# Window attention, forward and backward, on one core: transposes by DMA, shared score matmuls and a hand-ordered pipeline over four tiles

## The chip, the cores and the metric

The kernel runs on one core of one Trainium2 chip. The metric is the device time of the program in microseconds (us). The kernel before takes 3114.75 us (median of four runs, 3114.29 to 3115.95).

The engines are named as the profile names them: PE multiplies matrices (PEld is its weight loading), DVE and ACT do vector work, POOL and SP (SyncE) here mostly issue DMAs. "Evicting" a tile means copying a PSUM tile to SBUF, with a cast to bf16 where the PSUM tile is float32.

## The reference, cut to what matters

```python
# x, grad_out: (1, 256, 256, 384) bf16; wqkv: (384, 1152); wo: (384, 384); windows of 8 x 8 tokens
xw  = windows(x)                                  # 1024 windows of 64 tokens
q, k, v = split(xw @ wqkv)
p   = softmax(einsum('bqc,bkc->bqk', q, k) * 384**-0.5)
out = einsum('bqk,bkc->bqc', p, v) @ wo
# returned: out, and the gradients of x, wqkv and wo for grad_out
```

Both kernels fold the weights: with A = scale Wq Wk^T the scores are x A x^T, and with B = Wv Wo the output is P (x B). A tile is 128 tokens, that is two windows. Four tiles make a quad, and there are 128 quads. dS is the gradient of the scores, dP that of the probabilities. The weight gradients are accumulated as G and F from x^T U and x^T W, with U = dS^T x and W = P^T grad.

## The kernel before

The framework's scheduler orders the instructions of each engine. Per quad the kernel does this (cut):

```python
# x and grad of each tile are transposed on PE, and copied out of PSUM by DVE
for m in range(CK):
    nc.tensor.transpose(ps_xdT[:, 0, m*P:(m+1)*P], x_tok[:, m*P:(m+1)*P], ident[:])
for m in range(CK):
    nc.tensor.transpose(ps_xdT[:, 1, m*P:(m+1)*P], do_tok[:, m*P:(m+1)*P], ident[:])
nc.vector.tensor_copy(out=xdT_quad[:, :, :, bi*P:(bi+1)*P], in_=ps_xdT[:].rearrange(...))
# ... projections yT, xBT for the quad (512 columns), xBT transposed back on PE ...
for stage in (stage_f1, stage_f2, stage_b1, stage_b2, stage_b3):
    for bi in range(QUAD):
        stage(bi)          # softmax, output, dP, dS, U, W, one tile at a time
# stage_b3: dx of a tile, nine matmuls of 384 columns
for A_sb, srcT, o0 in ((A1_sb, uvwT_sb, 0), (A2_sb, uvwT_sb, P), (A3_sb, wT_sb, 0)):
    for mc in range(CK):
        nc.tensor.matmul(ps_dx[:], lhsT=srcT[:, mc, o0:o0+P], rhs=A_sb[:, mc, :], ...)
# ... after 16 tiles: G_acc and F_acc += x^T U, x^T W (ps_dw) ...
```

## Time and profile before

| what | value | view |
|---|---|---|
| span | 3115.0 us | page |
| PE / DVE / ACT busy | 98% / 65% / 49% | page, part 1 |
| PE's share of the chain that ended last | 88% | page, part 4 |
| one quad in the middle of the run | about 24 us | span over 128 quads, less the ends |

From the page: busy time and instructions of each engine, then two rows of the 40 time slices (the TensorE clock granted, and the busy share of the DMA engines, both in tenths).

```profile
PE 3041.1 (98%) x23935; PEld 1867.8 (60%) x23935; DVE 2020.5 (65%) x6758; ACT 1527.4 (49%) x3981; POOL 614.2 (20%) x1034
...
PEclk9999999999999999999999999999999999999999
DMA  4222222212222122222222221222212222222211
```

PE is nearly always busy and its clock is full. That alone does not say that PE is used well, because matmuls are pipelined and overlap. (The Trainium skill, "Trainium Kernel Development and Optimization", section "Performance Expectations", calls matmul busy time a bad metric for that very reason.) So look at the chain of waits, followed back from the last instruction, as shares of the span:

```profile
PE 88%; DVE 4%; issue 4%; ACT 3%; DMA 0%; ACTq 0%
```

At nearly every step PE's own previous matmul is what held the next one up. Two merged rows of the timeline (start, length, engine, line, operation, count) show its real pace:

```profile
1505.06 0.97 PE L316 MATMUL ps_dx<-A_sb,uvwT_sb 128*128 128x384 bf16 x5
...
1506.45 0.33 PE L210 MATMUL ps_xB<-ident,xBT_sb 128*128 128x128 bf16 x3
```

One matmul of 384 columns lasts 326 ns, but five take 0.97 us: they start (0.97 - 0.326) / 4 = 161 ns apart. Transposes of 128 columns start about 56 ns apart. These spacings, not the lengths, are what a removed matmul is worth. The transposes that the change moves to DMA stand in these groups (count, then busy us and mean ns of one, then the engine's idle time before them):

```profile
L180 PE MATMUL ps_xdT<-ident,x_tok 128*128 128x128 bf16 x1536 | 196.6, 219 | 2.2 <-DVE A_sb L118 0.3 <-DVE xdT_quad L183 0.3
L182 PE MATMUL ps_xdT<-ident,do_tok 128*128 128x128 bf16 x1536 | 185.5, 219 | 0.0
L183 DVE COPY xdT_quad<-ps_xdT 128x768 bf16<-128x768 bf16 x512 | 278.8, 549 | 6.9 <-PE ps_xdT L182 2.6
```

### The profile page before, as it was taken

Reading aid. Unit: us, or ns where it says so; the run is one execution under the profiler, and the core shown is the slowest. Engines: PE = TensorE matmul, PEld = TensorE weight load, DVE = VectorE, ACT = ScalarE, POOL = GpSimd, SP = SyncE. Lnnn points to the kernel's source line nnn. Section 1 sums busy time; section 2 is a strip of 40 time slices with the busy share of each in tenths; the row PEclk is TensorE's granted clock in tenths of the full one; section 3 lists DMA queues with packets and bytes.
Section 4 is the critical chain, followed back from the end, with each engine's and each line's share of the span. In section 5 each row is a group of like instructions: output and inputs, shape, how many; then the busy total and the mean of one; then the engine's idle time right before and its main releaser. Section 6 shows DMA issues by size and latency. Waiting matters only on the chain.

```text
span 3115.0 us, 64454 instructions
## 1 busy us (share of the span) xinstructions
PE 3041.1 (98%) x23935; PEld 1867.8 (60%) x23935; DVE 2020.5 (65%) x6758; ACT 1527.4 (49%) x3981; POOL 614.2 (20%) x1034
## 2 busy tenths in 40 slices
PE   8999999999999999999999999999999999999998
PEld 5565656666666656666566656566665656656564
DVE  6666766667666666666666666766666666667665
ACT  4445544445444454444554444544445444455443
POOL 4122111122111121111211212211112111121100
PEclk9999999999999999999999999999999999999999
DMA  4222222212222122222222221222212222222211
GB/s 129 68 63 64 71 69 69 70 52 76 68 70 69 52 76 69 70 68 60 65 71 70 71 66 54 76 68 70 70 53 74 68 70 69 62 65 71 58 33 40
DMA packets 206716, 208.43 MB, mean 67 GB/s; under 512 B 49216, under 2 KB 181056, under 8 KB 206400
## 3 DMA queue, kind: packets, MB, share of 16 engines
q0 software_dynamic: 65536, 101.25, 12.2%
q1 hardware_dynamic: 140464, 102.76, 11.2%
q8 instruction: 187, 3.06, 0.4%
q14 instruction: 129, 1.06, 0.1%
q10 hardware_dynamic: 400, 0.29, 0.0%
HBM read 101.84 MB, written 101.84 MB: 65 GB/s over the span
## 4 chain that ended last, share of the span: by engine, by line
PE 88%; DVE 4%; issue 4%; ACT 3%; DMA 0%; ACTq 0%
PE ps_dx L316 24%; PE ps_dw L331 13%; PE ps_p L190 8%; PE ps_p L196 8%; PE ps_t L300 5%; PE ps_W L282 4%; PE ps_w L305 4%; PE ps_xB L210 3%; PE ps_dP L259 3%; PE ps_U L277 3%; PE ps_S L216 3%; PE ps_out L248 2%; DVE xdT_quad L183 2%; PE ps_xdT L180 2%; PE ps_xdT L182 2%
## 5 line engine op out<-in xcount | busy, mean ns | idle before, releaser
L316 PE MATMUL ps_dx<-A_sb,uvwT_sb 128*128 128x384 bf16 x3072 | 703.6, 326 | 0.1
L175 POOL DMA_DIRECT2D do_tok<-in_grad_out_dram x512 | 300.6, 588 | 1429.1 <-PE ps_w L305 1247.3
L302 ACT CAST uvwT_sb<-ps_t 128x512 bf16<-128x512 f32 (+1 forms) x1024 | 498.9, 487 | 85.8 <-PE ps_t L300 82.4
L321 POOL DMA_DIRECT2D out_dram<-dx_sb x512 | 311.2, 608 | 1040.5 <-ACT dx_sb L320 1008.0
L284 DVE CAST W_sb<-ps_W 128x384 bf16<-128x384 f32 x512 | 284.2, 555 | 300.2 <-PE ps_W L282 295.4
L320 ACT CAST dx_sb<-ps_dx 128x384 bf16<-128x384 f32 x512 | 248.7, 486 | 391.1 <-PE ps_dx L316 327.4
L331 PEld LDWEIGHTS <-x_tok 128*128 128x128 bf16 x3072 | 296.5, 97 | 220.5 <-issue 49.2
L250 ACT CAST out_sb<-ps_out 128x384 bf16<-128x384 f32 x512 | 246.7, 482 | 357.1 <-PE ps_out L248 196.8
L316 PE MATMUL ps_dx<-A_sb,wT_sb 128*128 128x384 bf16 x1536 | 378.7, 328 | 0.0
L279 ACT CAST U_sb<-ps_U 128x384 bf16<-128x384 f32 x512 | 246.0, 481 | 268.5 <-PE ps_U L277 266.8
L196 PE MATMUL ps_p<-xdT_quad,Bm_sb 128*128 128x512 bf16 x1152 | 370.4, 379 | 0.1
L190 PE MATMUL ps_p<-xdT_quad,A_sb 128*128 128x512 bf16 x1152 | 364.3, 378 | 4.4 <-DVE xdT_quad L183 4.2
L224 ACT ACTIVATE pe<-ps_S,nmx 128x128 f32<-128x128 f32 x512 | 190.9, 373 | 320.4 <-DVE nmx L223 319.7
L300 PE MATMUL ps_t<-dSS_sb,x_tok 128*128 128x256 bf16 x1536 | 334.2, 272 | 1.0
L331 PE MATMUL ps_dw<-U_sb,x_tok 128*128 128x384 bf16 x1536 | 327.4, 325 | 0.6 <-DVE G_acc L333 0.6
L316 PEld LDWEIGHTS <-uvwT_sb 128*128 128x128 bf16 x3072 | 273.0, 97 | 90.8 <-issue 8.8
L307 DVE CAST wT_sb<-ps_w 128x384 bf16<-128x384 f32 x512 | 283.1, 553 | 46.8 <-PE ps_w L305 44.8
L192 DVE CAST yT_sb<-ps_p 128x512 bf16<-128x512 f32 x384 | 263.8, 687 | 58.2 <-PE ps_p L190 45.2
L198 ACT CAST xBT_sb<-ps_p 128x512 bf16<-128x512 f32 x384 | 229.5, 598 | 120.6 <-PE ps_p L196 117.3
L183 DVE COPY xdT_quad<-ps_xdT 128x768 bf16<-128x768 bf16 x512 | 278.8, 549 | 6.9 <-PE ps_xdT L182 2.6
L331 PE MATMUL ps_dw<-W_sb,x_tok 128*128 128x384 bf16 x1536 | 265.0, 325 | 1.4 <-DVE F_acc L333 0.8
L212 DVE COPY xB_sb<-ps_xB 128x384 bf16<-128x384 bf16 x512 | 181.4, 354 | 115.5 <-PE ps_xB L210 109.0
(93 smaller groups left out, 4732.5 us busy)
## 6 DMA issues: line engine op xcount, KB each, us to landing
x_tok<-in_x_dram SPq DMA_DIRECT2D x512, 96.0 KB
do_tok<-in_grad_out_dram POOLq DMA_DIRECT2D x512, 96.0 KB, 2.7
out_dram<-out_sb SPq DMA_DIRECT2D x512, 96.0 KB
out_dram<-dx_sb POOLq DMA_DIRECT2D x512, 96.0 KB, 2.5
w_sb<-in_wqkv_dram SPq DMA_DIRECT2D x1, 864.0 KB
out_dram<-dwqkv_sb SPq DMA_DIRECT2D x1, 864.0 KB
wo_sb<-in_wo_dram ACTq DMA_DIRECT2D x1, 288.0 KB
out_dram<-ep_t SPq DMA_DIRECT2D x1, 288.0 KB
```

The costliest lines, as they stand in the source:

```text
L175: nc.gpsimd.dma_start(out=do_tok[:], in_=dram_tile(grad_out, b, bt))
L183: nc.vector.tensor_copy(out=xdT_quad[:, :, :, bi * P:(bi + 1) * P], in_=ps_xdT[:].rearrange("p a (m t) -> p a m t", m=CK))
L190: nc.tensor.matmul(ps_p[:], lhsT=A2_sb[:, m, mq * P:(mq + 1) * P], rhs=xT_quad[:, m, :], start=(m == 0), stop=(m == CK - 1))
L192: (nc.scalar.copy if YT_ACT else nc.vector.tensor_copy)(out=yT_sb[:, mq, :], in_=ps_p[:])
L196: nc.tensor.matmul(ps_p[:], lhsT=Bm_sb[:, m, mco * P:(mco + 1) * P], rhs=xT_quad[:, m, :], start=(m == 0), stop=(m == CK - 1))
L284: nc.vector.tensor_copy(out=W_sb[:], in_=ps_W[:])
L300: nc.tensor.matmul(ps_t[:, i, :], lhsT=x_tok[:, mc * P:(mc + 1) * P], rhs=dSS_sb[:].rearrange("p a t -> p (a t)"), start=True, stop=True)
L302: nc.scalar.copy(out=uvwT_sb[:, mc0:mc0 + nm, :], in_=ps_t[:, 0:nm, :])
L307: (nc.scalar.copy if WT_ACT else nc.vector.tensor_copy)(out=wT_sb[:], in_=ps_w[:])
L316: nc.tensor.matmul(ps_dx[:], lhsT=srcT[:, mc, o0:o0 + P], rhs=A_sb[:, mc, :], start=(k == 0), stop=(k == 3 * CK - 1))
L321: nc.gpsimd.dma_start(out=dram_tile(out_1, b, bt), in_=dx_sb[:])
L331: nc.tensor.matmul(ps_dw[:], lhsT=x_toks[ti][:, ma * P:(ma + 1) * P], rhs=srcs[ti][:], start=(ti == 0), stop=(ti == GRP - 1))
```

## The change

The intent is to take work off PE and to give the rest a fixed rhythm.

- x and grad are transposed by DMA, SBUF to SBUF, one transpose of 128 x 1536 per quad and tensor, two quads ahead.
- A tile now covers 16 rows of 8 pixels, so its two windows are partitions 0 to 63 and 64 to 127. Scores and dP come from one set of matmuls: the stationary operand holds y and z (x A and grad B^T) of a window side by side, x^T of the window moves through it.
- Softmax and its gradient run over four tiles at once, in passes over half of the partitions.
- dx is three products per tile with operands projected beforehand (zq, yq, vq), in place of nine matmuls.
- PE, DVE and ACT keep a hand-written order: a step mixes quad `a` (projections, scores, softmax, token-major projections) with the attention products of quad `b` before it, and with "fillers", the matmuls of x^T U and x^T W.

The diff, cut to its core:

```diff
-                    for m in range(CK):
-                        nc.tensor.transpose(ps_xdT[:, 0, m * P:(m + 1) * P], x_tok[:, m * P:(m + 1) * P], ident[:])
-                    for m in range(CK):
-                        nc.tensor.transpose(ps_xdT[:, 1, m * P:(m + 1) * P], do_tok[:, m * P:(m + 1) * P], ident[:])
-                    nc.vector.tensor_copy(out=xdT_quad[:, :, :, bi * P:(bi + 1) * P],
+        for src, dst in ((dq, dT), (xq, xT)):
+            nc.sync.dma_start_transpose(out=dst[:].rearrange("p t m k -> p (t m) k"),
+                                        in_=src[:].rearrange("p t c -> p (t c)"))
 ... (cut: projections; y and z into one tile yz, a copy of z into zc) ...
+    def scores(st):
+                for m in range(CK):
+                    nc.tensor.matmul(sd[:, t, w, :],
+                                     lhsT=yz[:, m, t, 2 * w:2 * w + 2, :].rearrange("p s k -> p (s k)"),
+                                     rhs=xT[:, t, m, w * WT:(w + 1) * WT],
+                                     start=(m == 0), stop=(m == CK - 1))
 ... (cut: soft(0..5): max, shift, exp, sum and P, P*dP and its sum, dS) ...
+        wgt, dst, cp = ((B_sb, st["uq"], nc.vector.tensor_copy), (AT_sb, st["vq"], nc.scalar.copy))[part]
 ... (cut: yz_tok and turn, PE transposes of y, z, P and dS; attend; fillers) ...
-                for stage in (stage_f1, stage_f2, stage_b1, stage_b2, stage_b3):
-                    for bi in range(QUAD):
-                        stage(bi)
+    def step(a, b):
+        A(project, 0, 0)
+        B(0, 0)
 ... (cut: five more projections, each with one attention product) ...
+        filler(4)
+        A(scores)
+        A(soft, 0)
+        B(1, 2)
+        filler(2)
+        B(1, 3)
+        A(soft, 1)
+        A(uv, 0, 0)
+        B(2, 0)
+        A(soft, 2)
 ... (cut: soft 3 to 5 between uv and attention products) ...
+        A(turn, 0)
+        A(uv, 3, 0)
+        B(3, 2)
+        A(uv, 3, 1)
+        B(3, 3)
+        for t in range(QUAD):
+            A(yz_tok, t, 0)
+            filler(2)
+            A(yz_tok, t, 1)
+            filler(2)
+        A(turn, 1)
+        filler(2)
+    with tc.manual_schedule(engines=MANUAL):    # MANUAL = PE, DVE, Activation
```

## The prediction

> **What bounds the kernel now.** The page's first part gives PE 3041 of 3115 us (98%), DVE 2020, ACT 1527; the chain that ended last is 88% PE. Matmuls are pipelined, so I count streamed columns. The timeline shows five 384-column matmuls of ps_dx in 0.97 us, each 326 ns long: 161 ns from start to start. The Trainium skill, "TensorE: Matmul & The Clock Gate", section "Back-to-back issue gap", gives N/2.4 + 2.5 ns = 162.5; the trace agrees. Three 128-column transposes take 0.33 us, about 56 ns apart: weight loads are hidden. Granted clock: 0.999. Per quad of four tiles (128 quads) the kernel streams 50,688 columns in 186 matmuls: estimate 21.6 us. The middle of the trace takes 24.05 us per quad, so PE is 90% filled. DMA moves 67 GB/s, far from limiting.
>
> **PE, per quad.** Removed: 24 transposes of x and grad (now DMA), 12 of xB, the mask matmuls, 36 gradient matmuls of 384 columns, the transposed U/V/W products (12 of 256, 12 of 128). Added: 24 token-major projections of 384, 12 products of 384 into dx, 24 transposes of y and z. S and dP become 24 matmuls of 64 columns with 128-column weights, charged at 56 ns. Sum: 146 matmuls, estimate 18.7 us, 2.9 us less. All of it is on the critical path if PE stays the bound.
>
> **The second bound is DVE.** Softmax over four tiles at once cuts instructions (about 6750 to 4000), but half-partition passes, zc copies and yq/zq evictions come in. From durations of like instructions (0.555 us for a 128x384 float32 eviction, 0.354 for bf16, about 0.42 for a 256-column pass, interpolated from 0.285 at 128 columns and 0.556 at 384) I estimate 16 us per quad, as before (15.8), against 18.7 instead of 21.6. The order is fixed by hand. In the six projections ACT leads (5.6 us: six copies of 0.60, four of 0.48) and DVE mostly idles; then scores must end before softmax starts (2.2 us); then DVE has 14 us in a row, of which two PSUM buffers let about 1 us slip into the next step. Sum: 20.8 us per step. 129 steps and 55 us of start and end: about 2740 us.
>
> **DMA.** 256 transposes of 384 KB are added on SyncE's queue, which now spends 596 ns on each plain issue. The Trainium skill, "VectorE: DVE Perf Modes", section "The three transpose paths", gives 1309 ns for one 128x128: twelve in series, twice per quad, would be 31 us and near 4000 us in all. "DMA: Bandwidth & Descriptors", section "Latency and other measured facts", gives 261 GB/s: 1.5 us each, harmless. No trace here decides; I expect pipelining, nearer the second, hidden by the two-quad lookahead.
>
> **Predicted: 2740 us, 8 in 10 between 2570 and 3040.** Faster by over 2%: 0.82; within 2%: 0.05; slower: 0.13.
>
> **What would show it.** PE busy 85–92%; DVE 2000–2150 us busy, at least 75% of the span; the chain mixed PE/DVE/ACT, with softmax and eviction lines; PE waiting for DVE on uv, yz_tok and turn lines, for ACT in the projections; 64-column matmuls 56 ns apart; DMA share at most doubled; waits for xT or dT rare.
>
> **What would make it wrong.** Transposes that serialise, or block stores behind them on SyncE's queue (PE waiting on xT/dT, low clock in slices): slower. Half-partition passes over 0.42 us: up to 2900. DVE hidden better than I think: down to 2550.

## The result and the profile after

The changed kernel takes 2831.56 us (median of four runs, 2829.14 to 2835.57) against 3114.75 us. The ratio is 0.9092, with a 95% interval from 0.9079 to 0.9105. Ratios here are the mean time of one kernel's fast runs over the mean of the other's of the same rounds, so they are not quite the ratio of the medians. The outputs are correct.

The page of the changed kernel, the same lines as before:

```profile
PE 2485.4 (88%) x18814; PEld 1474.1 (52%) x18814; DVE 1976.6 (70%) x4899; ACT 1379.3 (49%) x2957; POOL 549.2 (19%) x1036
...
PEclk9999999999999999999999999999999999999999
DMA  6444444455444444445554444444445544444441
```

PE's busy time fell by 556 us, but the span by only 288: PE now idles. (Busy time counts overlapping matmuls, so here is a second count. Charge each matmul at the median distance between starts for its width in these traces: 29 ns for 64 columns, 56 for 128, 109 for 256, 162 for 384, 216 for 512. By this estimate the columns ask for 2775 us in the kernel before and 2324 us in the changed one. The rest of the time from PE's first start to its last, its pauses, grew from 329 to 492 us.) The chain that ended last has changed its nature:

```profile
PE 51%; DVE 43%; issue 3%; DMA 2%; ACT 1%; SPq 0%; ACTq 0%; DVEq 0%
```

To see how PE and DVE share it, take one step. The first projection of a quad begins a step, and its start can be read from the trace for every quad: the distance is 21.50 us in the median, and 117 of 127 distances are between 21.49 and 21.55 us. Here is the chain through one such step (start, length, link), cut. PE hands over to DVE at 1428.72. DVE keeps the lead until its accumulation (GF_acc) ends at 1440.49, with two short links of PE between (1431.15 and 1439.17); then PE leads to the next step.

```profile
1427.94 0.76 PE sd L161 x24
1428.72 0.43 DVE mx L174
...
1431.15 0.66 PE pj L216 x3
...
1437.49 0.56 DVE Wq L249
1438.05 0.33 DVE PT L233
...
1439.17 0.34 PE pt L224 x3
1439.53 0.36 DVE yq L225
1439.92 0.57 DVE GF_acc L274
1440.53 0.48 PE pw L271 x2
...
1443.54 0.65 PE pj L147 x3
```

The same step in three stretches: projections and scores, softmax, and the transposes of y and z with their fillers. Columns: stretch, its length, then busy us (and instructions) of each engine, the clock, the DMA share and GB/s.

```profile
core 0: us, PE busy (x) PEld busy (x) DVE busy (x) ACT busy (x) POOL busy (x), PEclk, DMA share, GB/s
1421.90:1428.70 6.80, 6.80 (x57) 3.76 (x56) 2.64 (x7) 4.80 (x10) 0.54 (x1) 1.00 0.43 90
1428.70:1437.90 9.20, 8.01 (x51) 4.61 (x50) 8.42 (x20) 5.95 (x13) 3.25 (x7) 1.00 0.33 95
1437.90:1443.40 5.50, 4.34 (x42) 3.01 (x42) 4.24 (x13) 0.00 (x0) 0.47 (x1) 1.00 0.07 19
```

In the first stretch PE never pauses and DVE works 2.6 of 6.8 us. In the second DVE hardly pauses (its gaps are short ones between passes, and 0.27 us of waiting for PE) and PE stands still for 1.2 us. In the third PE still waits twice for DVE, for PT and for the accumulation, and then sets the pace; the last 2.8 us are PE's without a pause. PE's timeline shows its two waits in brackets. It waits for PT because the transposes share two PSUM buffers, and the copy of PT has to empty one of them.

```profile
1438.44 0.33 PE L224 MATMUL pt<-ident,zc 128*128 128x128 bf16 x3 [0.97 <-DVE PT L233]
...
1440.53 0.48 PE L271 MATMUL pw<-Wq,xq 128*128 128x384 bf16 x2 [0.55 <-DVE GF_acc L274]
```

DVE's timeline shows its idle time in brackets: it waits for the attention product of tile 1 and then for the scores, and again for PE's transposes late in the step.

```profile
1427.33 0.56 DVE L249 CAST Wq<-pa 128x384 bf16<-128x384 f32 x1 [2.08 <-PE pa L248]
1428.72 0.88 DVE L174 TENSOR_REDUCE mx<-sd 64x4 f32<-64x256 f32 x2 [0.83 <-PE sd L161]
...
1437.97 0.42 DVE L233 COPY PT<-pt 128x512 bf16<-128x512 bf16 x1
...
1439.53 0.36 DVE L225 COPY yq<-pt 128x384 bf16<-128x384 bf16 x1 [0.15 <-PE pt L224]
...
1441.22 0.36 DVE L225 COPY yq<-pt 128x384 bf16<-128x384 bf16 x1 [0.48 <-PE pt L224]
...
1443.59 0.55 DVE L274 TENSOR_TENSOR GF_acc<-pw,GF_acc 128x384 f32<-128x384 f32 x1
```

And PE's waits over the whole run (total us, times, longest), cut. The rows for PT and uq are PE waiting for DVE. The row for vq is PE waiting for ACT, which in turn sometimes waited for a store to land before it could reuse an output buffer (last row).

```profile
PE pt L224 <- DVE PT L233: 94.8, 104, 1.3
...
PE pj L216 <- ACT vq L218: 72.6, 127, 2.7
PE pw L271 <- DVE GF_acc L274: 72.5, 132, 0.6
PE pj L216 <- DVE uq L218: 61.6, 217, 1.5
...
ACT osb L245 <- DMA out_dram<-osb: 52.2, 33, 2.8
```

The DMA transposes, from the view of their source line: the two groups, with the ns (min/median/max) that SyncE spends to issue one, then the time from issue to landing:

```profile
L136 SPq DMA_TRANSPOSE xT<-xq x128: 1413/1598/3337, 8.1 to 2714.8; - x128
L136 SPq DMA_TRANSPOSE dT<-dq x128: 1293/1459/3033, 21.0 to 2721.0; - x128
...
DMA to landing us min/median/max: 3.7/4.3/6.9
```

Twelve blocks of 128 x 128 land in about 4.3 us. Of the prediction's two estimates from the skill's figures, the one of blocks in series (31 us for the two transposes of a quad) does not come true; the measured time is nearer to the other. PE waited for a transposed tile once, at the start, for 6.2 us.

### The profile page after: what moved, and what is told of

Same layout as the page of the kernel before. It is cut to its first block, busy times and chain, and to the rows that moved or that the text cites. A ratio compares the mean times of both kernels' runs of the same rounds, so it can differ in the third digit from the quotient of the medians.

```text
span 2827.3 us, 50549 instructions
## 1 busy us (share of the span) xinstructions
PE 2485.4 (88%) x18814; PEld 1474.1 (52%) x18814; DVE 1976.6 (70%) x4899; ACT 1379.3 (49%) x2957; POOL 549.2 (19%) x1036
## 3 DMA queue, kind: packets, MB, share of 16 engines
q1 hardware_dynamic: 550064, 203.49, 34.2%
## 4 chain that ended last, share of the span: by engine, by line
PE 51%; DVE 43%; issue 3%; DMA 2%; ACT 1%; SPq 0%; ACTq 0%; DVEq 0%
PE pj L147 18%; PE pw L271 13%; DVE uq L218 9%; PE pt L224 5%; DVE sh L180 4%; DVE mx L174 4%; PE pj L216 3%; PE sd L161 3%; DVE pr L197 3%; DVE pd L204 3%; DVE yq L225 3%; DVE GF_acc L274 3%; DVE Wq L249 2%; DVE D L199 2%; DMA out_dram<-osb 2%
## 5 line engine op out<-in xcount | busy, mean ns | idle before, releaser
L150 ACT CAST yz<-pj 128x512 bf16<-128x512 f32 x384 | 227.1, 592 | 843.1 <-PE pj L147 843.1
L216 PEld LDWEIGHTS <-xT 128*128 128x128 bf16 x3072 | 299.2, 97 | 368.8 <-issue 200.4
L249 DVE CAST Wq<-pa 128x384 bf16<-128x384 f32 x512 | 283.4, 554 | 272.8 <-PE pa L248 268.8
L216 PE MATMUL pj<-B_sb,xT 128*128 128x384 bf16 x1536 | 333.3, 325 | 98.9 <-ACT vq L218 72.6
L271 PE MATMUL pw<-Wq,xq 128*128 128x384 bf16 x1536 | 364.2, 326 | 47.6 <-DVE GF_acc L274 47.6
L271 PE MATMUL pw<-Uq,xq 128*128 128x384 bf16 x1536 | 359.9, 326 | 24.9 <-DVE GF_acc L274 24.9
L216 PE MATMUL pj<-AT_sb,xT 128*128 128x384 bf16 x1536 | 334.6, 327 | 35.3 <-DVE uq L218 35.3
L147 PE MATMUL pj<-dT,BT_sb 128*128 128x512 bf16 x1152 | 316.0, 384 | 6.2 <-DMA dT<-dq 6.2
L218 DVE CAST uq<-pj 128x384 bf16<-128x384 f32 x512 | 284.5, 556 | 43.5 <-PE pj L216 35.5
L147 PE MATMUL pj<-xT,A_sb 128*128 128x512 bf16 x1152 | 311.3, 379 | 0.0
L224 PE MATMUL pt<-ident,zc 128*128 128x128 bf16 x1536 | 169.9, 220 | 95.5 <-DVE PT L233 94.8
L153 ACT CAST yz<-pj 128x512 bf16<-128x512 f32 x384 | 229.9, 599 | 16.4 <-PE pj L147 0.7
```

Source lines behind the costliest of these rows:

```text
L147: nc.tensor.matmul(pj[:].rearrange("p t w k -> p (t w k)"), lhsT=wgt[:, m, mo * P:(mo + 1) * P], rhs=src[:, :, m, :], start=(m == 0), stop ...
L216: nc.tensor.matmul(pj[:], lhsT=st["xT"][:, t, m, :], rhs=wgt[:, m, :], start=(m == 0), stop=(m == CK - 1))
L218: cp(out=dst[:, t, :], in_=pj[:])
L224: nc.tensor.transpose(pt[:, m, :], src[:, m, :, :].rearrange("p w k -> p (w k)"), ident[:])
L249: nc.vector.tensor_copy(out=st["Wq"][:, t, :], in_=pa[:])
L271: nc.tensor.matmul(pw[:], lhsT=st["xq"][:, t, ma * P:(ma + 1) * P], rhs=st["UW"[f] + "q"][:, t, :], start=(i == 0), stop=(i == n - 1))
```

## The experiments

**Order theory.** A step is a sum of parts. In each part one engine sets the pace while another idles, because the hand-written order puts the softmax of a quad right behind its own projections and scores: 6.8 us paced by PE, 9.7 us by DVE (from the first max at 1428.72 to the end of PT at 1438.39), 5.0 us by PE. (The chain above puts the second cut later: the first 2.1 of these 5.0 us are still mostly DVE's.)

**Queue theory.** Stores, loads and transposes share SyncE's queue. Stores come late, ACT waits for output buffers and PE for ACT.

**Stream theory.** PE's columns remain the bound, and the 88% is just what PE reaches.

All results below are correct unless said otherwise; each is the median of four runs.

| run | us | ratio to before |
|---|---|---|
| kernel before | 3114.75 | 1 |
| changed kernel | 2831.56 | 0.9092 |
| e2: no transposes (wrong results) | 2819.12 | 0.9049 |
| e3: uq evicted by ACT | 2645.63 | 0.8491 |
| e4a: extra DVE work, early | 2836.48 | 0.9104 |
| e4b: extra DVE work, late | 2874.70 | 0.9228 |
| e5: order left to the scheduler | 2570.21 | 0.8251 |
| e6: transposes back on PE | 3063.26 | 0.9835 |
| e7: kernel before, small DMA transposes | 3119.31 | 1.0015 |
| e8: rotated order | 2523.65 | 0.8101 |
| e9: rotated, uq on ACT | 2445.63 | 0.7848 |
| e10: rotated, uq on ACT, scheduler's order | 2429.67 | 0.7799 |
| e11: only PE's order left to the scheduler | 2612.73 | 0.8385 |
| e12: kernel before, DMA transposes per quad | 2873.53 | 0.9222 |

### e2: take the transposes away

```diff
+        if kept:
+            st["xT"], st["dT"] = kept
+            return
-        st["xT"] = xT = qp.tile([P, QUAD, CK, P], BF16, tag="xT", name="xT", bufs=3)
+        st["xT"] = xT = const.tile([P, QUAD, CK, P], BF16, name="xT")
 ... (dT likewise; kept holds the first quad's two tiles) ...
```

> Edit: the transposes are done for the first quad only and every quad reads those two tiles (wrong results on purpose; all other work, loads and stores stay). Order theory (a step is 6.8 us paced by PE, then 9.7 us paced by the hand-written DVE sequence, then 5.0 us paced by PE, and SyncE's queue is off the path): 2815 to 2832 us, and the 52 us that ACT waited for landed stores shrink or vanish without moving the time. Queue theory (transposes on SyncE's queue hold stores and loads up, ACT and then PE stall): faster by 50 us or more, at most 2780. Stream theory (PE's columns are the bound): unchanged.

Measured: 2819.12 us, 12 us faster, with wrong results as intended. ACT's wait for landed stores is gone from the list of waits, and the median step is still 21.49 us. So the queue cost the changed kernel about 12 us in all, not 50 or more. ACT's waits of 52 us were real, but other waits took their place: PE's wait for ACT's vq fell from 72.6 to 23.0 us, while its waits for PT rose from 94.8 to 125.7 and those for uq from 61.6 to 77.2. The queue theory falls as an explanation of the step.

### e3: move one eviction from DVE to ACT

```diff
-        wgt, dst, cp = ((B_sb, st["uq"], nc.vector.tensor_copy), (AT_sb, st["vq"], nc.scalar.copy))[part]
+        wgt, dst, cp = ((B_sb, st["uq"], nc.scalar.copy), (AT_sb, st["vq"], nc.scalar.copy))[part]
```

> Edit: the four evictions of uq per quad (0.556 us each on DVE) move to ACT, which idles half of the step. Order theory: the DVE-paced part loses about 4 x 0.48 us less what PE (8.0 us busy in it) and ACT (5.95 + 1.9) then need, so the step goes from 21.5 to 20.0-20.5 us: 2640 to 2710 us. Queue theory and stream theory: within 20 us of 2831.

Measured: 2645.63 us, 186 us faster from one changed word. The median step is 19.96 us, 1.54 less. PE streams exactly the same columns, so the stream theory falls: it allowed 20 us.

### e4a and e4b: the same useless DVE work in two places

```diff
+    def extra():
+        nc.vector.tensor_tensor(out=spare[:], in0=spare[:], in1=spare[:], op=ALU.add)   # 128x640 float32
 ... e4a:
         A(project, 1, 2)
+        extra()
         B(1, 1)
 ... e4b:
         A(soft, 2)
+        extra()
         A(uv, 0, 1)
```

> Edit: one useless DVE addition (128x640 float32, about 0.82 us) per quad after the last projection, where DVE idles 2.1 us before it can evict Wq of tile 1. Order theory: no change, within 12 us of 2831, though DVE is busier by about 105 us. A theory that DVE's total busy time sets the step: +105 us.

> Edit: the same useless DVE addition, but between the shift of the scores and the row sums, in the DVE-paced part. Order theory: +0.55 to 0.8 us per step (0.27 us of idle time nearby can absorb some): 2900 to 2935 us. Stream theory and queue theory: within 20 us of 2831.

Measured: early, 2836.48 us, which is 5 us more, and the intervals of its ratio and the changed kernel's overlap. The median step stays at 21.49 us, although DVE is busy 96 us longer. Late, 2874.70 us, 43 us more; the median step is 21.86 us. The direction is as the order theory says, the size is below what was expected (70 to 105 us). The timeline of e4b shows why:

```profile
1415.19 0.82 DVE L266 TENSOR_TENSOR spare<-spare 128x640 f32<-128x640 f32 x1
1415.92 0.55 DVE L249 CAST Wq<-pa 128x384 bf16<-128x384 f32 x1
1416.39 0.55 DVE L218 CAST uq<-pj 128x384 bf16<-128x384 f32 x1
```

The addition lasts 0.82 us, but the next instruction starts 0.73 us after it. And uq now follows Wq after 0.47 us, where in the changed kernel it followed after 0.82 us with 0.27 us of idle time. So 0.73 - 0.35 = 0.38 us should be left, and the step grew by 0.36. Work of an engine costs time where that engine sets the pace, and there at its spacing, not at its length.

### e5 and e11: leave the order to the scheduler

```diff
 ... e5:
-    with tc.manual_schedule(engines=MANUAL):
+    with ExitStack():
 ... e11:
-MANUAL = {mybir.EngineType.PE, mybir.EngineType.DVE, mybir.EngineType.Activation}
+MANUAL = {mybir.EngineType.DVE, mybir.EngineType.Activation}
```

> Edit: the block that keeps PE, DVE and ACT in hand-written order is dropped; the scheduler of the framework orders the same program. Comparing the two instruction orders, it differs only locally: two projection matmuls and a few fillers move into the place where PE waits for DVE's eviction of PT (0.97 us per step). Order theory: 0.3 to 0.9 us per step less, 2710 to 2800 us. A theory that holding the order by hand is itself the gain: slower than 2890 us.

> Edit: only PE's order is left to the scheduler; DVE and ACT keep the hand-written one. Dropping all three gave 2570 us where 2710 to 2800 was expected. If the gain came from PE filling its waits with other matmuls: 2560 to 2680 us. If it came from DVE's and ACT's order (row sums and reciprocal spread between evictions): 2780 us or more.

Measured: e5 takes 2570.21 us. That is 261 us less than the changed kernel and far below the expected 2710 to 2800: a miss in size. The program is the same; only the order of its instructions differs, and only locally: in the traces all but 12 of PE's 18814 matmuls stand within 40 places of where the hand order has them. e11, with PE alone set free, takes 2612.73 us, so PE's order alone brings 219 of the 261 us (84%); DVE and ACT run exactly the sequence of the changed kernel there. The third stretch of a step in e5 shows the difference:

```profile
1401.37 0.98 PE L271 MATMUL pw<-Uq,xq 128*128 128x384 bf16 x5
1402.79 0.33 PE L224 MATMUL pt<-ident,zc 128*128 128x128 bf16 x3 [0.45 <-DVE PT L233]
1402.96 0.33 PE L271 MATMUL pw<-Uq,xq 128*128 128x384 bf16 x1
1403.12 0.59 PE L147 MATMUL pj<-dT,BT_sb 128*128 128x512 bf16 x2
1403.55 0.33 PE L224 MATMUL pt<-ident,yz 128*128 128x128 bf16 x3
```

Five fillers instead of two run before PT is needed, and the wait for it is 0.45 us instead of 0.97. L147 is the first projection of the next quad: it runs where PE waited for the accumulation, and by the time the next step begins, a part of it is done. The hand order allows no such overlap between steps. My expectation counted the 0.97 us at PT alone. PE's lists of waits show what it left out: from the changed kernel to e5 the wait for PT falls from 94.8 to 57.1 us, but the one for the accumulators also falls from 72.5 to 4.5, and the one for ACT's vq from 72.6 to 0.6; the one for uq stays (61.6 and 62.5). These add up to 178 of the 261 us; the rest is not in single rows of the lists, and no run separates the shares.

### e6: undo the DMA transposes

```diff
-        for src, dst in ((dq, dT), (xq, xT)):
-            nc.sync.dma_start_transpose(...)
+    def tran(st, t, which):
+        for m in range(CK):
+            nc.tensor.transpose(pt[:, m, :], src[:, t, m * P:(m + 1) * P], ident[:])
+        nc.vector.tensor_copy(out=dst[:, t, :, :], in_=pt[:])
 ... (called for the next quad after B(0, 0), B(0, 1), B(0, 2), B(0, 3)) ...
```

> Edit: undo one part. x and grad of the next quad are transposed on PE (24 matmuls of 128 columns per quad) and evicted by DVE (8 evictions of 0.354 us) in the projection part, where DVE idles; no DMA transposes. Order theory: that part is paced by PE, so it grows by 24 x 56 ns = 1.34 us to 2 us per step: 3000 to 3090 us, so that DMA transposes are worth 60 to 90% of the whole gain. Theory that transposes on SyncE's queue cost as much as they save: within 30 us of 2831.

Measured: 3063.26 us, 232 us slower; the median step is 23.44 us, 1.94 more, within the expected 1.34 to 2. In the changed kernel the DMA transposes are worth 232 of its 283 us of gain.

### e7 and e12: the DMA transposes alone, in the kernel before

```diff
 ... e7: per tile, 128x384, two buffers
+                    nc.sync.dma_start_transpose(out=xT_quad[:, bi, :, :], in_=x_tok[:])
+                    nc.sync.dma_start_transpose(out=doT_quad[:, bi, :, :], in_=do_tok[:])
 ... e12: per quad, 128x1536, three buffers; the quad's tiles lie side by side
+                for src, dst in ((dq, doT_quad), (xq, xT_quad)):
+                    nc.sync.dma_start_transpose(out=dst[:].rearrange("p t m k -> p (t m) k"),
+                                                in_=src[:].rearrange("p t c -> p (t c)"))
 ... both: the PE transposes and their DVE copies are removed ...
```

> Edit: one part of the change alone. The kernel before, but with x and grad transposed by DMA (one transpose of 128x384 per tile and tensor) instead of 24 PE transposes and four DVE copies of 128x768 per quad. If the kernel before was bound by PE's streaming: 24 x 56 ns x 128 = 172 us less, 2920 to 2980 us. If it was bound by waits between engines: under 60 us less, or nothing. If 1024 small transposes clog SyncE's queue: slower than 3115 us.

> Edit: the kernel before with DMA transposes again, now one per quad and tensor (128x1536, as in the changed kernel) and three buffers in place of two. With one transpose per tile and two buffers PE was busy 155 us less but waited 197 us for transposed tiles. If small transposes and the short lookahead were the reason: 2920 to 3000 us. If SyncE's queue order (stores and transposes in one line) is: 3060 us or more.

Measured: e7 gains nothing, 3119.31 us. Where did the saved work go? First part of its page:

```profile
PE 2885.9 (92%) x20863; PEld 1712.1 (55%) x20863; DVE 1804.1 (58%) x6246; ACT 1495.1 (48%) x3981; POOL 614.9 (20%) x1034
```

The longest entry for transposed tiles in its list of PE's waits (total us, times, longest):

```profile
PE ps_p L184 <- DMA xT_quad<-x_tok: 197.1, 50, 9.5
```

PE is busy 155 us less than before and waits 197 us for transposed tiles, up to 9.5 us at a time. A second loss shows in the clock: 0.967 was granted in e7, and 0.997 in e12. The clock record of e7's trace has 37 stretches at half clock, 204 us in all. Of the 36 after the start, 35 begin during or just after a pause of PE of 2.2 us or more, and in them matmuls of 384 columns start 320 ns apart instead of 162. By my estimate from these distances that costs about 68 us. e12 has the same work, with larger transposes and one more buffer, and takes 2873.53 us, faster than the expected 2920 to 3000:

```profile
PE 2820.7 (98%) x20863; PEld 1688.1 (59%) x20863; DVE 1815.4 (63%) x6246; ACT 1497.4 (52%) x3981; POOL 615.6 (21%) x1034
```

PE is back at 98%, and 241 us are gone. That is 85% of what the whole change gained, from one part of it. PE's spacing accounts for 24 x 56 ns x 128 = 172 us. The rest is pauses of PE: counted as above, they are 329 us before and 258 us in e12. That they shrink because the DVE copies and their PSUM buffers went too is likely but not shown. e12 changed the size of a transpose and the number of buffers together, so which of them mattered is open.

### e8, e9 and e10: another order

```diff
     def step(a, b, n):                      # n: the quad after a
+        A(scores)
+        A(soft, 0)
+        N(project, 0, 0)
+        B(0, 0)
+        filler(2)
+        A(soft, 1)
+        N(project, 0, 1)
 ... (cut: soft 2 to 4 between the projections of n) ...
+        A(turn, 0)
+        A(uv, 0, 0)
+        B(1, 2)
+        A(soft, 5)
 ... (cut: uv, attention products, copies into zc; then yz_tok with fillers) ...
-    AHEAD = 2
+    AHEAD = 3
 ... (more buffers for xq, dq, xT and dT; the final tiles share buffers to make room) ...
 ... e9: as e8, and uq evicted by ACT; e10: as e9, without the hand-held order ...
```

> Edit: the same instructions in another hand-written order: a step begins with the scores of its quad, and the projections of the NEXT quad run on PE while DVE does this quad's softmax; fillers end their accumulations at points where no filler follows at once; one more quad is loaded ahead. Order theory (the three parts of a step are paced by different engines in turn, and each idles meanwhile): with DVE 15.4 us and PE 17.8 us of work per step now overlapping, a step takes 18.5 to 19.5 us: 2440 to 2570 us. Stream theory or queue theory: 2800 us or more.

> Edit: the rotated order with uq evicted by ACT. The rotated kernel still showed PE waiting 0.48 us per step for DVE's uq and 0.23 us for the accumulators. Order theory: PE is nearly the bound at 18.2 us of streaming; a step falls from 19.2 to 18.5-18.9 us: 2430 to 2490 us. If ACT (then about 13.2 us per step) becomes the new wait: 2520 us or more.

> Edit: as the run before, but the framework's scheduler orders PE, DVE and ACT, as it did in the kernel whose hand-held order was dropped (2570 us). Order theory: what is left of waits is small, so the scheduler can add little or take little: 2400 to 2500 us. If the scheduler undoes the rotation by its own idea of readiness: about 2570 us.

Measured: 2523.65, 2445.63 and 2429.67 us, each as expected of the order theory. e8 does the same arithmetic as the changed kernel on the same engines and is 308 us faster, because DVE's softmax now runs beside the projections of the next quad. (e8 also loads one quad further ahead, with more buffers. No run tests that alone; but the changed kernel waited for a transposed tile only once, so it can hardly be the cause.) Its median step is 19.21 us; e9's is 18.60 and e10's 18.53. In e10 PE is busy 99%, as the first part of its page says:

```profile
PE 2394.9 (99%) x18814; PEld 1454.4 (60%) x18814; DVE 1703.5 (70%) x4387; ACT 1566.6 (65%) x3469; POOL 549.0 (23%) x1036
```

Its list of PE's waits has two single ones at the start as the longest in total:

```profile
PE pj L147 <- DMA dT<-dq: 8.2, 1, 8.2
PE pt L78 <- DMA w_sb<-in_wqkv_dram: 6.8, 1, 6.8
PE pw L273 <- DVE GF_acc L276: 3.9, 7, 0.6
```

This is the version that beats both kernels: 22% under the kernel before and 14% under the changed one (2429.67 / 2831.56 = 0.858). It is again bound by PE's columns, as the kernel before was, only with fewer of them: of 2416 us from PE's first start to its last, 2324 us are columns, counted as above.

## Why the prediction was right or wrong

The time was predicted at 2740 us with a range of 2570 to 3040, and 2831.56 was measured: inside the range, faster as forecast, 91 us above the point.

- **The bound before: right.** The kernel before was bound by PE's columns. e12 takes columns away, leaves the order to the same scheduler, and the time falls by 241 us, of which 172 are the columns' own. Counted as above, columns were 89% of PE's time before, as the prediction said (90%).
- **PE's new sum, 18.7 us per step: nearly right, a little high.** e10 runs a step in 18.53 us. One term was mis-sized: the 24 score matmuls, charged at 56 ns each, take 31 ns each, as this row of the changed kernel's timeline shows: (0.91 - 0.193) / 23 = 31 ns, where 193 ns is the length of one. With it the sum is 18.1 us.

```profile
1427.78 0.91 PE L161 MATMUL sd<-xT,yz 128*128 128x64 bf16 x24
```

- **DVE as second bound, half-partition passes of 0.42 us: right.** They take 0.415 to 0.422 us, and DVE's work in the step shown is 15.3 us (predicted 16). DVE was busy 1976.6 us, just under the predicted 2000 to 2150, but that is 70% of the span and not at least 75%.
- **The 20.8 us of a step: the step that failed.** The prediction was "then DVE has 14 us in a row, of which two PSUM buffers let about 1 us slip into the next step", 13 us in all. Measured: 14.7 us from the first max to the next step. DVE's work was near the estimate: 13.4 us busy from the first max to the end of its last accumulation at 1444.14, and 0.8 us of that do slip into the next step. What failed is "in a row": DVE idles 2.0 us in between, 1.1 of them waiting for PE. Among the transposes of y and z the two wait for each other: PE waits for PT (0.97 us in the step shown), DVE then waits for PE (0.15 and 0.48 us), and PE for the accumulators (0.55 us). When DVE has ended that accumulation, PE still has 2.8 us of its own to the next step.
- **"In the six projections ACT leads (5.6 us ...) then scores must end before softmax starts (2.2 us)": wrong, in the other direction.** PE led and never paused; projections, fillers and scores took 6.8 us, not 7.8. The two errors leave 0.7 us: 21.5 instead of 20.8, and 0.7 x 128 = 90 us is the whole miss. That it is so small is partly luck: one error is 1.0 us too much, the other 1.7 us too little. ACT, named as a part of the chain and as what PE would wait for in the projections, has 1% of the chain.
- **DMA: right.** Transposes land in about 4.3 us, the DMA engines' share doubled from about 0.24 to 0.47 in the windows of the middle, and waits for xT or dT are rare. The queue I named as a risk cost 12 us (e2).
- **What the prediction did not ask: whether the hand-written order was good.** It took the order's idle times as the price of the rewrite. e5 shows that this price, 261 us, was nearly as large as the whole gain, and that the scheduler's order did not pay it. The saving of columns had all been there (e10). Counted as above, the columns fell by 451 us, and PE's pauses rose by 163 to 492 us under the hand order; with the same columns they are 232 us in e5 and 92 in e10.

## What to carry to other kernels

Moving transposes from a bound PE to DMA was most of the gain here, but only with large transposes, enough buffers and a lead: the same removal with small ones and two buffers gained nothing. When two engines are each busy 70 to 90%, lay one step out as a sequence, ask of each part which engine sets its pace, and put another quad's work beside it; an order that makes a quad wait for itself adds the engines' times instead of overlapping them. Before you hold an order by hand, run the same program with the scheduler's order: it is one line, and here it was worth 261 us, nearly as much as the whole rewrite (283 us). On the better hand order it was worth only 16 us (e10 against e9).

## What the Trainium skill lacked or had wrong

- "VectorE: DVE Perf Modes", section "The three transpose paths", gives 1309 ns for a DMA transpose of one 128x128 block and does not say what several in one instruction cost. Here twelve blocks in one instruction landed in 4.3 us (median), 0.36 us a block.
- "DMA: Bandwidth & Descriptors", section "Latency and other measured facts", gives 261 GB/s for a DMA transpose with a non-contiguous middle dimension, and more for a contiguous one. Here the hardware queue took 34.2% of 2827.3 us with the transposes and 13.7% of 2815.5 us without (e2). The difference, 581 us of all 16 engines for 99.9 MB more, is about 172 GB/s, beside other traffic.
- No page gives the time that SyncE spends on issuing one transpose of this size ("DMA: Bandwidth & Descriptors" has cycle counts of other sizes alone): 1.46 to 1.60 us in the median here, against 0.596 us for a plain transfer of 96 KB in the kernel before.
- "TensorE: Matmul & The Clock Gate", section "Back-to-back issue gap", gives a floor of about 25 ns for matmuls of up to 64 columns, or about 62 ns when the sequencer decodes them. Here 64-column matmuls, each with fresh 128-column weights, started 31 ns apart, which is near the first figure. For a stream with new weights for each matmul the section gives longer spacing at 128 columns (81 ns) and shorter at 512 (131 ns) than its formula; here, also with new weights for each, the medians are 56 and 216 ns, which is what the formula gives.
